# A fused attention and two-layer kernel: the hand-written order of the first half's instructions is replaced

## The chip, the cores and the metric

The kernel runs on one core of one Trainium2 chip. Its time is the device time of one execution in microseconds (us); where several runs were made, their median is compared. A core has five instruction streams that matter here: TensorE (PE; its weight loads are shown as PEld), VectorE (DVE), ScalarE (ACT), GpSimd (POOL) and SyncE (SP), which issues every DMA of this kernel. Each engine takes its own instructions strictly in their order and waits on semaphores for the others.

## What is computed

From the reference, cut to what matters:

```python
# q, k, v: (8, 8, 576, 64); keys and values are averaged over groups of 8 rows
k_p = k.reshape(B, H, 72, 8, D).mean(axis=3)
v_p = v.reshape(B, H, 72, 8, D).mean(axis=3)
attn = softmax(q @ k_p.T / sqrt(D))
x = (attn @ v_p)                 # as 4608 tokens x 512
h = x @ w_in                     # 512 -> 1024
solu = h * softmax(h)
ln = (solu - mean) / sqrt(var + 1e-6) * g_ln
x2 = ln @ w_out                  # 1024 -> 512
h2 = x2 @ w_in2                  # 512 -> 2048
out = (h2 * sigmoid(h2)) @ w_out2    # 2048 -> 512
```

All of it is float32. The kernel splits each float32 operand of a product into a high part, rounded for TensorE's fast format, and a low part (the remainder), and sums three products: high with high, high with low, low with high. The three projections after the hidden layer are done by a seven-product scheme on 2 x 2 blocks, which needs sums and differences of blocks beforehand.

## The kernel before

The 4,608 tokens are 36 tiles of 128. In the **first half** a tile passes through scores, softmax, transposed probabilities, attention, the hidden layer, its normalisation, a transpose and (by groups of four tiles) the first output projection. The weights are unpacked, scaled and split into high and low parts in the same stretch. The **second half**, from the function `window` (L1107) on, is the last two projections; its order comes from loops with slot numbers and is not touched here.

The order of the first half is written out by hand in a text, `SCRIPT` (L62 to L215): 2,881 words, and `run` (L1476) goes through them. A word names a piece of work and its place, such as `S3` (scores of tile 3). Each function behind a word is a generator; each time its word comes up, it emits its next piece, mostly one instruction or a few on one engine, and stops. Since all five engines are under `manual_schedule` (L1439), the instructions of each engine are run in just the order in which the words emitted them. Between engines only the data, the buffers and the semaphores order them. A suffix chooses the engine of that piece where there is a choice: `/1` VectorE, `/2` ScalarE, `/3` GpSimd; without one the piece's default stands (`pick`, L279).

The words (L1468) that the prediction speaks of, with their pieces:

- `W` (warm, L1442): that many pairs of 128x128 filler matmuls on TensorE, whose result nobody reads. `W29` is 58 instructions, `W14` 28, `W6` 12, `W4` 8, `W9` 18.
- `L` (L1347) loads a row of w_in (512 KB), `l` (L1336) unpacks it: ScalarE, then ScalarE or VectorE, VectorE, the high part, the low part. `H` needs it.
- `k` (prep_k, L400): the load of keys (SP; for batch 0 one load of 576 KB serves two head pairs, else 288 KB each), the sum over groups of 8 (VectorE one reduction, or GpSimd three adds, `pool_sum` L386), and scaled copies into `kbd`, two for each of the four head pairs. `v` (L427) and `r` (L455) do the same for the values; loads of batch 0 are 512 and 384 KB, else 256 and 192.
- `q` (L489): the load of one tile's queries (256 KB) into one of three buffers. A buffer is free again when the scores of its tile are done.
- `S` (scores, L496): eight matmuls (sixteen where a tile crosses a batch), then the row maximum on VectorE.
- `X` (softmax, L521): four pieces of two exponentials on ScalarE, a scale, a reciprocal on VectorE, the probabilities `pb` and `lf` (GpSimd by default, or VectorE).
- `T` (L560): transposes on TensorE and the split into high and low. `a` (attend, L606): the attention products, and the split of their result into `xTh` and `xTl`.
- `H` (hidden1, L643): three matmuls of 512 columns. `M` (L665), `E` (L674), `Z` (L689): maximum, exponential, product and mean, variance and scaling; GpSimd has one piece in `E` and two or three in `Z`. `N` (L718): the transpose back.
- `R` (operand1, L746): a difference where the scheme needs one (VectorE or GpSimd), the high part (any of three engines) and the low part `np` (VectorE or GpSimd), for each of two halves. `P` (project1, L790): twice 12 matmuls, then an eviction on VectorE.
- `o` (L1397) and `w` (L331): unpacking of the other weights. `c` (L1448) and `d` (L1456): the first operands of the second half, tokens and weights. `f` (first_pair, L1072): the second half's first seven products and their evictions.

One queue issues all loads and stores in the script's order: a load that waits for its buffer holds back every later one. Keys and values of batches after the first share three raw buffers (`RAWS`, L216).

Of the kernel before, what the change touches and what calls it, by code (L numbers as in the profile page):

```python
# [74 lines left out]
X5 X4 T4 T4 v1,3 T3 r1,1 H1,0,2 X5 T3 k2,2 H1,0,0 T3 q7 T4/1 X5 H1,0,1 T3 k2,0 k2,1/3 X5 o0
S6 v2,0 X5 v2,1 o0 X5 H1,0,3 w0 S6 q8 H1,1,1 X5 T4 T4 X6 T4 E0 H1,1,3 X6 k2,2 H1,1,0 X6 o0
k2,3 H1,1,2 X6 o0/1 a2 a2 M1 o0 o0 a2 o0/3 a2 a2 a2 E1 o0/3 a2/1 a2 a2 S7 o0/3 Z0 E1 a2 q10
o0 S7 a2 o0/3 a2 a2 a2 H2,0,1 a2 H2,1,0 o0 T4/1 H2,1,2 T4 T4 X7 X7 Z0 k2,3 H2,0,2 X6 X7 Z0
a2 v2,2 H2,1,3 r1,1 v2,0 X7 H2,1,1 E1 v2,1 v2,3 Z0/2 H2,0,0 r1,1/1 o0/1 o0/3 o0 r1,1/2
H2,0,3 Z1 Z1 o0/1 T5 o0/3 o0/1 X6 M2 N0 o0/3 N0 N0 X6 o1 E2 T5 T5/1 r2,0 T4 T5 X6 T6 E2 T6  # L80
o0 T6 S8 X7 Z1 o0 T6 H3,0,2 k2,3/2 N0 S8 H3,0,0 E2 Z1 Z2 T6/1 H3,0,1 v2,3 Z2 H3,1,2 v2,2 T5
k3,0 o1 r1,1 r2,0 H3,1,1 k3,1 o0/3 k2,3/2 T6 o1 H3,1,0 k3,2 Z2 q11 X8 H3,0,3 o1 X8 H3,1,3
o1/1 o1 N0 Z2 T5 X8 a3 a3 M3 X8 N1 v2,3 k3,0/3 N1 N1 a3/1 N2 k3,1 E3 S9 k3,2/3 r2,1 r1,1/2
r1,1/1 a3 a3 a3 v3,0 E3 N2 X8 a3 k3,3 X8 a3 a3 a3 a3 E3 X8 Z3 a3 a3 a3 H4,1,2 H4,0,0 a3/1 Z3
a3 N1 H4,1,3 v2,3 S9 v2,3 H4,0,2 o1 Z3 X8/1 o1/1 H4,1,1 X9 X7 r2,1 w2 H4,0,3 X9 X7 k3,3 v3,1
Z3/2 H4,0,1 o1 k4,0 H4,1,0 X9 X7 T7 M4 X9 v2,3 N2 T8 o1/3 T8 k3,3/1 N2/1 o1 o1 E4 v3,0/3 T7
# [1562 lines left out]
```

## Time and profile before

| | |
|---|---|
| median of 3 runs | 1278.84 us (1278.65 to 1280.33) |
| the profiled execution | 1281.28 us |
| its span, first to last instruction | 1279.5 us |
| mean granted TensorE clock | 0.993 |
| PE busy | 1242.0 us (97%), 7,292 matmuls |
| DVE busy | 1016.8 us (79%) |
| ACT busy | 794.1 us (62%) |
| POOL busy | 480.7 us (38%) |

Busy time is the union of the instructions' spans on an engine. In a timeline a row merges equal instructions in a run (x8), and gives in brackets how long the engine was idle before it and what released it. A wait for several semaphores is put down to the one that came last. PEclk is the TensorE clock that was granted, as a share of 2.4 GHz; 0.5 is 1.2 GHz. "m" are products of the second half's first projection, "op" of its second, "hp" hidden, "sp" scores, "av" attention, "xq" the first output projection, "np" its operands.

### The profile page before, as it was taken

Reading aid. Unit: us, or ns where it says so; the run is one execution under the profiler, and the core shown is the slowest. Engines: PE = TensorE matmul, PEld = TensorE weight load, DVE = VectorE, ACT = ScalarE, POOL = GpSimd, SP = SyncE. Lnnn points to the kernel's source line nnn. Section 1 sums busy time; section 2 is a strip of 40 time slices with the busy share of each in tenths; the row PEclk is TensorE's granted clock in tenths of the full one; section 3 lists DMA queues with packets and bytes.
Section 4 is the critical chain, followed back from the end, with each engine's and each line's share of the span. In section 5 each row is a group of like instructions: output and inputs, shape, how many; then the busy total and the mean of one; then the engine's idle time right before and its main releaser. Section 6 shows DMA issues by size and latency. Waiting matters only on the chain.

```text
span 1279.5 us, 21818 instructions
## 1 busy us (share of the span) xinstructions
PE 1242.0 (97%) x7292; PEld 1131.2 (88%) x7292; DVE 1016.8 (79%) x1719; ACT 794.1 (62%) x1949; POOL 480.7 (38%) x655
## 2 busy tenths in 40 slices
...
GB/s 283 215 174 262 215 297 241 247 242 217 195 215 154 99 149 91 201 128 206 281 282 275 231 347 299 239 241 206 367 343 393 329 280 282 254 277 264 197 286 143
DMA packets 139410, 308.69 MB, mean 241 GB/s; under 512 B 12032, under 2 KB 63232, under 8 KB 137760
## 3 DMA queue, kind: packets, MB, share of 16 engines
...
q8 instruction: 58, 0.95, 0.3%
...
## 4 chain that ended last, share of the span: by engine, by line
PE 52%; DVE 2%; DMA 1%; issue 0%; SPq 0%; ACT 0%; DVEq 0%; ACTq 0%
PE m L1057 27%; PE op L1300 24%; DVE gr L851 1%; PE xq L799 1%; DMA gr<-gd 1%; DVE gt L851 1%; SPq L1217 0%; DVE w2s L851 0%; DVE ob L1333 0%; DVE t L851 0%; DVE np L292 0%; ACT gt L1280 0%; ACT np L285 0%; DVE lnr L759 0%; DVE xo L807 0%
## 5 line engine op out<-in xcount | busy, mean ns | idle before, releaser
L1057 PE MATMUL m<-t,w2s 128*128 128x384 f32 x2016 | 351.9, 335 | 2.1 <-DVE gb L1068 2.1
L1057 PEld LDWEIGHTS m<-t,w2s 128*128 128x128 f32 x2016 | 351.0, 189 | 2.8 <-DVE gb L1068 2.4
L1300 PE MATMUL op<-gt,w2o 128*128 128x512 f32 (+1 forms) x1680 | 346.2, 368 | 0.7 <-DVE gt L851 0.5
L1300 PEld LDWEIGHTS op<-gt,w2o 128*128 128x128 f32 x1680 | 292.4, 189 | 54.4 <-DVE gt L851 2.2
L1280 ACT ACTIVATE gt<-gr 128x512 fp32r<-128x512 f32 (+1 forms) x240 | 139.8, 588 | 144.6 <-PE op L1300 55.8
L851 DVE TENSOR_TENSOR gt<-gr,gt 128x512 fp32r<-128x512 f32 (+1 forms) x240 | 155.4, 654 | 61.4 <-ACT gt L1280 57.9
L656 PE MATMUL hp<-w1ih,xTh 128*128 128x512 f32 x288 | 118.7, 412 | 2.7 <-DVE e L681 2.5
L799 PE MATMUL xq<-np,w1p 128*128 128x256 f32 x864 | 113.3, 284 | 4.2 <-DVE np L292 2.8
L656 PE MATMUL hp<-w1ih,xTl 128*128 128x512 f32 x288 | 113.5, 394 | 0.4 <-DVE xTl L292 0.4
L799 PEld LDWEIGHTS xq<-np,w1p 128*128 128x128 f32 x864 | 106.7, 189 | 7.6 <-DVE np L292 4.0
L656 PE MATMUL hp<-w1il,xTh 128*128 128x512 f32 x288 | 112.9, 392 | 0.1
L526 ACT ACTIVATE pr<-sp,st 128x72 f32<-128x72 f32 x288 | 88.6, 329 | 20.7 <-DVE st L517 14.2
L799 PE MATMUL xq<-np,w1o 128*128 128x256 f32 x648 | 84.5, 284 | 2.4 <-DVE np L292 1.1
L799 PEld LDWEIGHTS xq<-np,w1o 128*128 128x128 f32 x648 | 80.1, 189 | 5.4 <-DVE np L292 2.0
L851 POOL TENSOR_TENSOR tt<-x2r 128x768 f32<-128x768 f32 x22 | 44.6, 2028 | 98.0 <-DMA x2r<-x2d 64.9
L851 DVE TENSOR_TENSOR gr<-gr 128x512 f32<-128x512 f32 (+1 forms) x120 | 80.1, 669 | 0.2
L292 POOL TENSOR_TENSOR np<-lnr,np 128x512 fp32r<-128x512 f32 x43 | 60.2, 1401 | 43.1 <-ACT np L285 23.6
L292 DVE TENSOR_TENSOR np<-lnr,np 128x512 fp32r<-128x512 f32 x83 | 65.1, 792 | 10.7 <-ACT np L285 7.2
L656 PEld LDWEIGHTS hp<-w1ih,xTl 128*128 128x128 f32 x288 | 54.2, 188 | 13.1 <-DVE xTl L292 1.1
L1068 DVE TENSOR_TENSOR gb<-m,u 128x384 f32<-128x384 f32 x48 | 26.7, 556 | 49.1 <-ACT u L1124 31.9
L656 PEld LDWEIGHTS hp<-w1ih,xTh 128*128 128x128 f32 x288 | 54.5, 189 | 12.2 <-DVE e L681 4.6
L1068 DVE TENSOR_TENSOR ga<-m,u 128x384 f32<-128x384 f32 x47 | 26.1, 555 | 49.3 <-PE m L1057 49.0
...
## 6 DMA issues: line engine op xcount, KB each, us to landing
...
```

Of the source, the lines that this page charges most:

```text
L292: pick(1).tensor_tensor(lo, src, hi.bitcast(F32), op=ALU.subtract)
L526: nc.scalar.activation(pr[:, g, h], sv[:, g, h], AF.Exp, bias=st[:, 0, g, h : h + 1], accum_out=st[:, 1, g, h : h + 1],)
L656: nc.tensor.matmul(hp[:, f], l, r, start=(n == 1 and m == 0), stop=(n == KC and m == 2))
L799: nc.tensor.matmul(hq[:, b], w[:, k, l], t[:, k % 2, r], start=(b == k == i == 0), stop=(k == 3 and i == 2), skip_group_check=True,)
L851: eng.tensor_tensor(dst, a, b, op=ALU.subtract)
L1057: nc.tensor.matmul(to, wt[:, a, o : o + P], tk[:, b, k], start=(start and k == 0 and m == 0), stop=(k == 1 and m == 2), skip_group_check=n ...
L1068: eng.tensor_tensor(dst, a, b, op=ALU.add)
L1280: nc.scalar.activation(ring[m][:, 0], src, AF.Copy)
L1300: nc.tensor.matmul(acc[c, x][d], w[:, l, P * d : P * d + P], t[:, r], start=(first and f == i == 0), stop=(f == NF - 1 and i == 2), skip_g ...
```

## The change

Only the text of `SCRIPT` is replaced. The new one has 2,881 words too, and each word without its suffix comes up as often as before; the order and the suffixes differ nearly everywhere. The first eight lines and the last two of either text:

```diff
 SCRIPT = """
-L0,0 k0,0 W14 L0,2 k0,2 q0 L0,1 q1 q6 W6 l0,0 L0,3 W29 k0,0 k1,0 l0,0/1 k0,1 l0,2 k0,1/3
-k0,1/1 l0,0 l0,2/1 k0,0/1 k0,0 l0,2 k0,2 l0,2 k0,3 k0,2 k0,2/1 k0,3/1 k0,3/3 S0 l0,1 S0 q2
-k1,1 S1,1 l0,0/1 X0 v0,0 l0,1/1 v0,2 l0,2 X0 W4 r0,0 S1,1 L1,3 X0 X0 l0,0 v1,0 X1 l0,1 X1
-l0,1/1 q3 l0,1 X0 X1 S2 k1,0 X1 X0 v1,1 X1 X0/1 l0,3 L1,2 X0 W9 L1,0 S2 v0,0/3 k1,1 X2 v0,2
-X2 v0,1/3 T0 X2 r0,0 k1,2 T0 T0 r0,1 k1,0/3 X2 X1 L1,1 r0,1/1 v0,3 r0,1 X2 l1,3 w0 X1 T0
-l1,3 S3 r0,1/2 X1 l1,3 l0,3 v0,3/1 r0,1/1 v0,3/1 v0,3 l0,3 l1,2 a0 v0,3 S3 T0 r0,1/2 r0,1/2
-l1,3/3 T0 a0 X3 v1,0 v1,1/3 l0,3 a0/1 k1,3 k1,2 k1,0 o0 a0 a0 a0 q4 k1,2/3 l1,3 q5 l0,3/3
-a0/1 v1,2 a0 a0 a0 a0 X3 v1,3 a0 a0 a0 T1 T1 T1 l1,0 a0/1 H0,0,2 X2 a0 X2 l1,1 l1,1/1 a1 T1
...
-d d d P8,7 R8,4 R8,3 R8,3 R8,3 P8,3 R8,4 R8,4/3 R8,4 P8,5 R8,4 P8,3 d R8,4 P8,4 P8,7 P8,7
-P8,4 P8,3 P8,3 f P8,4 d P8,4 f f d d f f f c f f f f f f f f f f
+L0,0 k0,0 W29 k0,2 q0 q1 L0,1 L0,2 v0,0 l0,0 l0,0/1 v0,2 k0,0 q6 k0,0/1 k0,0 l0,0 k0,3 k0,2/3
+k0,1 k0,1 k0,1/3 k0,2 k0,3/1 k0,3/1 k0,2/1 S0 l0,0/1 l0,0/3 S1,1 l0,1 S0 q2 k1,0 W14 X0 L1,3
+l0,1/1 r0,0 l0,1 X0 k1,1 l0,2 l0,2/1 l0,1/3 X0 v0,0 q3 l0,1/3 X0 v0,1 W6 S1,1 X0 L1,0 X0 l0,2 X1
+X0 v0,2 X1 S2 L1,1 X1 k1,0 k1,2 X0 W4 X1 l0,2/3 S2 k1,0 T0 X1 l1,3 X1 L0,3 T0 v0,3 X1 W9 X2 r0,0
+v1,0 X2 k1,0/3 v0,3/3 r0,1 o0 X2 v0,3 X2 X1 l1,3/1 r0,1 S3 X2 v0,3 T0/1 r0,1 l1,3 a0 r0,1 k1,1
+l1,3 X2 v0,3/1 k1,3 X2 T0 T0 r0,1/2 l1,1 q4 L1,2 r0,1/2 T0 a0 r0,1/2 l1,3/3 S3 l1,1 a0 k1,2 a0
+a0 a0 a0 X3 v1,1 l1,1 a0 a0 a0 a0 l0,3 l1,1/3 l0,2 l0,3 X2 v1,0 l1,1/3 l0,3 v1,2 a0 a0 a0 T1 T1
+H0,0,2 T1 X3 T1 T1 a0 X3 a1 l0,3/3 T1 a1 X3 k1,3 l0,3/3 l1,0 a1/1 v1,3 a0 l1,0 a1 a1 a1 v1,1
...
+P8,2 d d d R8,7 P8,7 D8,2,1 R8,3/3 P8,6 R8,4 P8,7 R8,3 R8,3 R8,3 P8,3 R8,4 R8,4 R8,4/3 R8,4 R8,4
+P8,4 P8,5 d P8,3 d d P8,7 P8,4 P8,7 P8,3 P8,3 P8,4 f c P8,4 f f d c c f f f f f f f f f f f f f
 """
```

At the front, `W14` and `W6` go from ahead of `W29` to behind `S0`, one of batch 0's key sums (`k0,2/3`) goes to GpSimd, and the second key load, the query loads and the value loads `v0,0` and `v0,2` come earlier in SP's order than the third and fourth rows of w_in. Over the whole text the low part of `R` is on GpSimd 53 times of 126 (43 before), the probabilities `pb` 30 times of 36 (26 before), the sums in `k` 8 times of 32 (5 before), those of the main values in `v` 4 times of 32 (11 before); the first copies of `T` and `a` go to ScalarE 71 times of 128 (59 before). At the end, three pieces of `c` instead of one come behind the first `f`.

## Rows read from the trace of the kernel before

**Rows 1.** The chain that ended last, in order of time: start us, us, what.
```profile
562.17 0.60 DVE w2r L851
...
594.78 335.00 PE m L1057 x1920
...
965.45 311.03 PE op L1300 x1529
```

**Rows 2.** Timeline, 574 to 600 us: start us, us, engine line op out<-in.
```profile
575.78 16.89 PE L1057 MATMUL m<-t,w2s 128*128 128x384 f32 x96
575.98 0.69 DVE L807 TENSOR_TENSOR xo<-xq,xo 128x512 f32<-128x512 f32 x1 [0.63 <-PE xq L799]
...
579.17 0.95 DVE L851 TENSOR_TENSOR t<-tt,t 128x768 fp32r<-128x768 f32 x1
```

**Rows 3.** Stretch, us; busy PE, PEld, DVE, ACT, POOL (instructions); PEclk, DMA share, GB/s.
```profile
14.00:50.00 36.00, 26.70 (x156) 23.02 (x155) 28.79 (x59) 26.13 (x116) 21.38 (x33) 0.81 0.79 256
50.00:178.70 128.70, 118.68 (x670) 98.84 (x671) 120.51 (x254) 115.68 (x408) 104.35 (x211) 1.00 0.69 219
178.70:534.30 355.60, 349.13 (x2391) 319.06 (x2390) 311.96 (x544) 207.06 (x579) 211.09 (x302) 1.00 0.60 192
534.30:575.80 41.50, 37.43 (x294) 34.95 (x293) 38.03 (x55) 21.10 (x35) 17.53 (x19) 1.00 0.45 147
```

**Rows 4.** Timeline, 0 to 34 us (PEld is the weight load beside PE).
```profile
1.86 12.92 PE L1445 MATMUL idle<-ident 128*128 128x128 f32 x98 [1.86 <-POOL ident masks.py:199]
...
5.83 0.75 DVE L388 TENSOR_REDUCE kp<-early 128x72 f32<-128x576 f32 x1 [5.83 <-DMA early<-kT]
...
11.68 0.42 DVE L398 TENSOR_SCALAR kbd<-kp 64x72 f32<-64x72 f32 x2
...
14.61 2.13 PE L507 MATMUL sp<-kbd,q 128*128 128x144 f32 x16
15.79 0.33 SPq L491 DMA_DIRECT2D q<-qT  x1
...
29.85 2.26 PE L507 MATMUL sp<-kbd,q 128*128 128x144 f32 x8 [6.54 <-DMA q<-qT]
...
32.34 0.48 PE L618 MATMUL av<-pth,vbh 128*128 128x128 f32 x1 [0.24 <-ACT vbh L285]
```

**Rows 5.** What SP's queue waited for, 0 to 60 us: total us, times, longest.
```profile
SPq L491 <- PE sp L507: 6.9, 2, 6.5
```

**Rows 6.** Busy us in stretches of 4 us at the start, as rows 3.
```profile
0.00:4.00 4.00, 2.14 (x10) 2.15 (x11) 0.00 (x0) 1.28 (x1) 3.43 (x13) 1.00 0.53 160
4.00:8.00 4.00, 4.00 (x31) 4.00 (x31) 2.03 (x5) 1.54 (x3) 0.43 (x2) 1.00 1.02 417
8.00:12.00 4.00, 4.00 (x38) 4.00 (x37) 3.86 (x11) 1.52 (x4) 0.19 (x1) 1.00 1.05 406
12.00:16.00 4.00, 4.00 (x37) 4.00 (x37) 0.31 (x2) 0.00 (x0) 0.05 (x1) 1.00 0.30 111
...
24.00:28.00 4.00, 0.00 (x0) 0.00 (x0) 1.34 (x3) 2.37 (x14) 3.04 (x7) 0.74 1.02 315
```

**Rows 7.** VectorE and GpSimd groups, 0 to 600 us: busy us, mean ns
```profile
L292 DVE TENSOR_TENSOR np<-lnr,np 128x512 fp32r<-128x512 f32 x83 | 65.1, 792 | 10.7 <-ACT np L285 7.2 <-POOL np L289 2.5
...
L292 POOL TENSOR_TENSOR np<-lnr,np 128x512 fp32r<-128x512 f32 x43 | 60.2, 1401 | 43.1 <-ACT np L285 23.6 <-DVE np L287 18.7
...
L538 POOL TENSOR_TENSOR pb<-pr,st 128x512 f32<-128x512 f32 x26 | 28.0, 1075 | 11.1 <-DVE st L534 6.2 <-PE pm L566 2.0 <-PE xq L799 1.5
...
L392 POOL TENSOR_TENSOR raw<-raw 128x288 f32<-128x288 f32 x5 | 4.0, 800 | 0.2
...
L392 POOL TENSOR_TENSOR raw<-raw 128x144 f32<-128x144 f32 x5 | 2.3, 451 | 0.4
...
L392 POOL TENSOR_TENSOR kp<-raw 128x72 f32<-128x72 f32 x5 | 2.0, 393 | 0.4
```

**Rows 8.** Waits, 0 to 580 us: total us, times, longest.
```profile
ACT sqd L693 <- POOL ls L685: 18.0, 15, 2.3
```

More of the change, by code (lines that the diff above doesn't have):

```diff
@@ L75 @@
[L75 to L86, printed above, removed]
@@ new lines @@
+H2,1,1 o0/1 Z1/2 o0/1 o0/3 N0 M2 T4 T5 N0/1 N0 S8 X6 T4 o0 o0/3 o0/3 o0 o0/3 o1 E2 X6 T5 r2,0 N0
+E2 k3,0 X7 T5 X6 T6 w0 T6 k2,3 S8 H3,0,2 T6 o0 X7 v2,3 r1,1/2 H3,1,2 E2 r1,1 T6 T6 X8 k3,1
+H3,0,0 o0/3 w1 T5 T5 Z2 H3,1,1 Z2 T5 k2,3 H3,1,0 o0/3 o1 o1/1 H3,1,3 T6 X8 o1 H3,0,1 X8 k3,0
+H3,0,3 o1 o1 a3 r1,1/1 r1,1 X7 k3,2 a3 Z2 X7/1 q11 M3 N1 a3 N0 X8 r2,0/3 a3 k3,1/3 r2,1 N1 N1 E3
+a3 a3 S9 a3/1 a3 a3 a3 E3 N1 Z2/2 v2,3/3 k3,3 a3/1 N1 v2,3 X8 a3 a3 a3 T7 T7 H4,1,2 o1 q12 X8 E3
+k3,2 a3 H4,0,0 X8 Z3 S9 H4,0,2 v3,0 Z3 a3 H4,1,3 X9 Z3 o1/1 H4,1,1 v2,3 T7 o1 H4,0,3 X9 r2,1
@@ new lines @@
+Z7 k4,3/1 o2 H8,1,0 S14 N6 T12 o2 H8,0,0 o2 o2/3 Z7 T11 o2 w3 H8,0,1 k5,0 X13 X14 H8,1,1 T11
+k5,2 Z7 X14 H8,1,2 N6 r4,1 X13 H8,1,3 o2 o2/1 T11/1 T12 T12 o2 X14 T12 X13 N7 X14 M8 N7 X13 T13
+T12 T13 o2/3 T11 T13 S15 T13 o2/3 k5,2 N7 o2/3 o2 T13 E8 T12 T13 N7 o2/3 a6 E8 a6 w3 o2 o3 X14
+a6 v5,0 o2/1 w4 E8 v5,1 w3 q17 a6 a6 a6 H9,1,3 a6 H9,1,1 Z8 Z8 w3 X14 S15 H9,0,3 q18 X14 N3
+H9,0,0 X15 o2 H9,0,2 X15 Z8 k5,1 X15 H9,1,0 a6 o3 o3/1 H9,0,1 Z8/2 o3 H9,1,2 o3/3 o3 v5,2 w5 a6
+X15 a6 M9 a6 a6 a6 a6 S16 E9 v4,3/1 w4/1 v4,3 N8 w6 v4,3 E9 N8 v4,3 a6 N8 r3,1 w4 H10,0,1 N8 E9
@@ new lines @@
+v5,0 H10,1,2 X14 Z9 S16 Z9 k5,3 H10,0,3 o3 H10,0,2 o3/1 r3,1/1 T13 Z9 v5,1 H10,1,0 X15 X16 a6
+k6,0 H10,0,0 o3 N7 H10,1,3 Z9 q19 v5,2 w7 T13 T13 X16 X16 H10,1,1 w5 k6,1 X15 T13 X15 X16 T14
+M10 N9 T14 T14 X15 T15 T14 E10 S17 T14/1 N9 T15 E10 q20 o3 N9 r3,1/2 X16 S17 H11,0,0 X17 o3/1
+o3/3 k5,3/3 o3/3 E10 k5,3 H11,0,3 o3/1 X17 o3 H11,0,2 o3 o3/3 T15/1 w5 H11,1,0 o3/3 X16 X17 T15
+H11,1,1 o3 N9 T15/1 X16 H11,1,2 T15 w6 v5,3 w8 X17 H11,1,3 w5 w4 H11,0,1 T14 X17 Z10 Z10 r3,1
+X16 a7 a7 M11 o3 Z10 o3/1 o3 a7 E11 a7 a7 a7 S18 o3 q21 X17 a7 E11 X17 o3 o3 o3 E11 o3/3 o3/1
@@ new lines @@
+a8 Z14 N13/1 a8 a8 Z14 X20 R2,4 T18 T18 r5,1 H15,1,1 a8/1 v5,3/3 v6,2 H15,1,2 a8 X20 S22 H15,1,3
+N13 X20 M15 P2,3 v5,3 v5,3 T18 v5,3 T18 T18 w11 N13 X22 R2,7 T19 T18 D3,1,0 w11 P2,3 R2,7 r4,1/1
+r4,1/1 r4,1/1 P2,7 D3,1,1 R3,1/3 w11 w14 T19 T19 X22 E15 T19 X21 X22 X22 P2,7 X21 X22 T19 w13
+w13/1 E15 v6,0 E15 S23 w12 w13 w15 R2,4 k7,0 v6,1 H16,0,0 q25 Z15 Z15 X21 R2,4 H16,1,0 R2,4
+H16,1,1 Z14/2 Z15 w12/1 H16,1,2 v6,2 w16 R2,4 H16,1,3 R3,1 Z15/2 R2,4/3 P2,7 N14 H16,0,1 N14
+P2,7 w14 H16,0,2 X22 S23 N14 R3,1/1 P2,4 w12 R3,1/3 P2,3 w14 w12 w13 X23 P2,4 v6,3 w14 X23 w17
@@ new lines @@
+k6,3/1 P2,3 N15 P2,4 R3,2 H16,0,3 N15 N14/1 P2,4 N15 q26 R3,2 R3,2 P3,1 X23 r6,0 R3,5/3 M16 X23
+a9 P3,1 T19 E16 R3,2 r5,1 a9 N15 P3,2 E16 w15 w15 a9/1 P3,1 P3,2 w18 R3,5/1 w14 R3,5 R3,5/3
+R3,5/3 k6,3 r5,1 r5,1/2 X23 D3,4,0 w15 R3,6/3 D3,4,1 v6,3 a9 a9 a9 S24 a9/1 R3,5/3 H17,0,0 X23
+a9 P3,2 a9 a9 E16 a9/1 k7,0/3 a9 a9 a9 T20 T20 S24 T20 H17,0,1 Z16 a9/1 H17,1,0 X23 T20 T21
+T20/1 R3,6 r5,1 H17,0,2 a9 T20 T21 T21 w18 H17,1,1 X22/1 X22 X23 H17,0,3 r5,1/1 X24 T21 R3,6/3
+T22 T21/1 T22 T21 T22 H17,1,2 X24 T22 R3,6/3 H17,1,3 T22/1 X24 T22 a10 X24 a10 M17 Z16 P3,5 a10
@@ new lines @@
+R3,4/1 Z18 T23 X25 H19,0,1 S26 X25 H19,1,0 T23/1 X26 Z18 H19,1,1 T23 R4,1 X25 H19,0,2 X26 R3,4
+X26 R3,4 H19,1,2 X26 H19,0,3 R3,4/1 u1,0 Z18 r6,1 q29 N17 H19,1,3 v7,0 w20 R3,4 v7,1 P3,4 r6,1
+M19 Z18/2 w20 R4,1 P3,4 E19 T23/1 w22 R4,1/1 w17 w20 N18 P3,3 R4,1/3 E19 S27 N18 P4,1 R4,2/1 E19
+P3,4 Z19 Z19 S27 P3,4 H20,0,0 w20 a10 X27 H20,1,0 R4,2 R4,2/3 Z19 X27 P4,1 T23 w19 Z19/1 w19
+R4,2 N18 X27 w23 H20,1,1 k7,3 v6,3 X27 N19 v6,3 N18/1 v7,2 P4,2 w21 v6,3/3 w19 v6,3 N19/1 w21
+P4,2 P4,1 R4,5 D4,4,0 R4,5 N19 R4,5/3 R4,5 D4,4,1 T24 N19 q30 T24 T24/1 X26 H20,0,1 R4,5/3
@@ new lines @@
+R6,3 R6,3 X35 R6,7 H29,1,2 r7,1/1 P6,6 R6,3/3 X35 H29,1,3 X35 H29,0,0 R6,4/3 r7,1/2 Z28/2 P6,3
+R6,7 T32/1 T33 P6,5 D7,1,0 H29,0,2 R6,7 H29,0,3 R6,7/1 P6,3 M29 R6,7/3 T32 E29 r7,1 N28 D7,1,1
+r7,1 P6,7 X35 N28 E29 P6,7 X34 E29 v7,3 T33 T33/1 X35 T33 H30,0,0 X35 T33/1 N28 T33 r7,1 P6,7
+H30,0,1 N28 X34 Z29 a15 P6,7 a15 P6,3 H30,0,3 Z29 a15 P6,3 a15 a15 a15 H32,0,0,1 R6,4/1 a15
+R6,4/3 R6,4 a15 a15 a15 u0,0 a15/1 a15 a15 a15 T34 Z29 H32,0,1,1 X34/1 T34 T34/1 T35 T34 T34
+Z29/2 H30,1,0 T34 H30,1,1 X35/1 R6,4/1 T35 T35 T35 H30,1,2 R6,4/3 T35/1 H30,1,3 T35 H30,0,2 a16
@@ new lines @@
+a16 M30 H32,1,0,1 N29 a16/1 E30 H32,0,2,1 a16 N29 N29 E30 a16 H32,1,1,1 a16 a16/1 E30 Z30 Z30
+a16 a16 a16 H31,0,0 a16/1 H31,1,0 a16 N29 R7,1/1 a16 a16 Z30 H31,0,1 a16 a16 a15 H31,1,1 a15 c
+H31,1,2 c c Z30/2 H31,1,3 c P6,4 c c c H31,0,2 H32,0,3,1 w30/1 c N30 H31,0,3 R7,1 R7,1/3 P6,4
+R7,1/3 M31 P7,1 E31 R7,2/1 w30 c w30 R7,2/3 R7,2/1 P7,1 E31 N30/1 H32,1,2,1 E31 Z31 Z31 P6,4
+H32,1,3,1 R7,2 P6,4 N30 M32 Z31 P7,2 c E32 H33,0,0 D7,4,0 c H33,1,0 E32 P7,2 Z31/1 H33,1,1 E32
+D7,4,1 Z32 N31 H34,0,0,1 N31/1 H34,0,1,1 P7,1/1 N31 H34,0,2,1 N31 R7,5 H33,0,1 R7,5/1 H33,0,2
@@ new lines @@
+R7,5 R7,5/3 H33,0,3 R7,5/1 P7,2 R7,5/3 H33,1,2 N30/1 H33,1,3 R7,6 H34,1,0,1 R7,6 H34,1,1,1
+R7,6/3 R7,6 M33 R7,6 P7,5 E33 R7,6/3 P7,5 D7,2,0 R7,7 P7,2 Z32 E33 P7,6 R7,3 D7,2,1 Z32 P7,6
+R7,3/3 R7,3/1 R7,3 Z32/2 E33 H34,1,2,1 P7,6 R7,7 H34,1,3,1 Z33 Z33 R7,7/3 R7,7 H34,0,3,1 R7,7
+P7,3 M34 c Z33 R7,7 P7,7 D0,1,0 P7,5 Z33/2 R7,4 P7,7 c c P7,3 R7,4/3 R7,4/3 R7,4 P7,7 R7,4 N32
+P7,3 D0,1,1 H35,0,0 N32 P7,7 R7,4 R0,1 N32 u0,1 P7,4 E34 R0,1 R0,1/1 N32/1 P7,4 E34 R0,1 P0,1
+E34 R0,2/1 Z34 Z34 P7,4 P0,1 R0,2 P7,4 R0,2 R0,2 P0,2 c R0,5 P0,2 D0,4,0 R0,5/1 P0,1 R0,5/3 R0,5
```

211 lines of the change are left out of this document (81 added, 130 removed).

## The prediction

> **What bounds the kernel now.** I read the chain of work that ended last first [rows 1]. Followed back from the last instruction it reaches no further than 562.17 us, and from 594.78 us on it is TensorE almost without a break: 335.00 us of the first projection's products, then 311.03 us of the second's. The script doesn't order that half, so it can only move the moment at which the half begins (the first pair's products, 575.78 us, [rows 2]), and the rest moves with it.
>
> Ahead of that moment the stretches have different limits [rows 3]. From 14 to 50 us no engine is full: VectorE works 28.79 of 36 us, TensorE 26.70. From 50 to 178.7 (attention, hidden layer and weight preparation at once) VectorE is at 120.51 of 128.7 (94%), ScalarE at 115.68, GpSimd at 104.35 (81%). From 178.7 to 534.3 TensorE is at 349.13 of 355.6 (98%), and in the last 41.5 us VectorE (38.03) and TensorE (37.43) share the limit. TensorE's idle time between 50 and 575.8 us is 10.0 + 6.5 + 4.1 = 20.6 us.
>
> The start loses most. TensorE spends 12.92 us from 1.86 on 98 filler matmuls, and the scores of tile 0 start behind them at 14.61 [rows 4]. Their last operand, a scaled key copy on VectorE, was done at 11.68 + 0.42 = 12.10, so the filler outlasted the data by 2.5 us. The next query load on SP's queue needs the buffer that those scores free: it goes out at 15.79, after a wait of 6.5 us [rows 4, 5]. Behind it every other load stands, and the DMA engines run dry: from 12 to 16 us they are busy 0.30, at 111 GB/s against 417 from 4 to 8 [rows 6]. The hole is (1 - 0.30) x 4 = 2.8 us. Later tile 3's scores wait 6.54 us for their queries and start at 29.85; from 24 to 28 us TensorE does nothing, VectorE only 1.34 us, and the granted clock averages 0.74, between its two levels of 2.4 and 1.2 GHz, after TensorE had stood idle. The first attention product starts at 32.34 [rows 4, 6].
>
> **The change part by part.** Both scripts have 2,881 words and the same pieces; only their order and the engine suffixes differ. TensorE's work and SP's transfers keep their sums, so a gain is less waiting and nothing else.
>
> *Filler.* W29 (58 matmuls) now stands alone ahead of S0; W14 and W6 (40) stand between S1 and S2. Ten matmuls run in the first 4 us, 31 in the next 4, then 38 in 4, which is 0.105 us each [rows 6]: 58 end at 8 + 17 x 0.105 = 9.8 us. The data: the second key load is third in SP's queue instead of fourth, with one load of 0.52 MB less ahead, 1.3 us at 417 GB/s. The first key sum began when its load had landed, at 5.83 [rows 4]; 0.59 MB later, at about 7.2, the second lands. One of its two sums goes to GpSimd, three adds of 0.800 + 0.451 + 0.393 = 1.64 us [rows 7], to 8.9; VectorE does three sums of 0.75 from 5.83 on with a weight piece between them, to about 9. With the scaled copies of 0.2 each, S0 starts at about 10.1, 4.5 us sooner. If the data came no sooner than before (12.10) it would be 2.5; if the filler alone held it, 4.8. I take 4.5, since the order of the loads is written out.
>
> *SP's queue.* Ten loads stand ahead of q2 in either order, 4.36 MB before and 4.59 MB now (from the shapes). With 0.64 MB moved in the first 4 us (160 GB/s) and 410 GB/s after, 4.59 MB last until about 13.6 us; q2 goes out at about 11.3, so the hole of 2.8 us closes. The first values (v0) now stand ahead of q2, and q3 is the 16th load with 6.62 MB up to it, not the 18th with 7.40: another 1.9 us. Of tile 3's wait of 6.54 us most should go. Late next is VectorE, busy 28.79 of the 36 us: the stretch can shrink beyond the shift by nothing, or by all its idle time, 7.2 us. I take 2.0, three quarters of its one clear gap (4 - 1.34 = 2.66 us at 24 to 28), since the other gaps are waits on one another. With the shift: **-6.5 us**, ends -2.5 and -12.0.
>
> *Engines changed.* Ten low parts of projection operands go from VectorE to GpSimd (53 there, not 43): -10 x 0.792 = -7.9 us on VectorE, +14.0 on GpSimd [rows 7]. Four scalings of probabilities go the same way: +4.3 on GpSimd (1.075 each), some -3 on VectorE. Seven value sums come back and three key sums go, net four off GpSimd at about 1.64: -6.6, and +3.0 on VectorE. Sums: VectorE about -8, GpSimd +11.7; the other moves nearly cancel. The relief is worth at most VectorE's share in the stretch where it is fullest, 8 x 128.7 / 525 = 2.0 us. GpSimd covers its load even if all of it fell there: 104.35 + 11.7 = 116 of 128.7. If that cover is gone and every moved low part stands on the path, the cost is 10 x (1.401 - 0.792) = 6.1 us. I take 0, ends -2.0 and +6.1.
>
> The row has a low part on GpSimd at 1.77 times VectorE's time, and the rule speaks against the move: the Trainium skill, GPSIMD Engine Reference, section 4.1, keeps elementwise work on VectorE and calls GpSimd about twice as slow with two inputs. By its factor the ten would cost 7.9 us on the path, and the sum would be +1.4 instead of -6.5.
>
> *The order from 50 to 575.8 us.* Here an order can win at most TensorE's 20.6 idle us. Counted in the two scripts, TensorE pieces with a direct producer at most two words ahead fall from 42 to 27, at most four from 62 to 56. That lengthens leads a little; what it is worth no row tells, and the words' spacing is a plan. I take 0, ends -5 and +5, a quarter of the idle time.
>
> *The end.* The low part of T3 now stands behind the first pair's first product. The fourth product needs it, 18 matmuls in, at 575.78 + 18 x 16.89 / 96 = 578.9; VectorE has it after its last eviction (576.7) and 0.95 us [rows 2], at 577.6. It is covered by 1.3 us: 0, or 0.95 if the cover is gone.
>
> **Sum:** -6.5 us. The profiled execution took 1281.28 us (span 1279.5, 1.8 around it), 2.4 above the median of the runs, 1278.84 (1278.65 to 1280.33). Taken off the median it gives **1272.3 us**; a profile as far above the median would show about 1274.8. A measurement of this kernel tells about 0.2%, 2.6 us, from no change.
>
> **Rivals.**
> *The whole start is won* (1266.8): the stretch up to 50 us also loses all of VectorE's idle time, -12.0. For it: tile 3's queries were 6.54 us late and attention begins only at 32.34. Against: VectorE is in demand from 28 us on.
> *Better on average, not on this chip* (1278.8): the order was made for scattered durations, and this kernel has one set of them. The dense stretch takes the 6.5 us back. It spends 128.7 us where its fullest engine works 120.51, so 6.5 more of waiting is possible. Against: its leads are as long as before, and DMA, which keeps its own time, is busy only 0.69 of that stretch [rows 3].
> *GpSimd late for every tile, slower* (1284.9): each of the 36 tiles passes GpSimd three times, for the mean, the variance and the scaling, and ScalarE already waits there 18.0 us in 15 waits for the mean [rows 8]. In GpSimd's queue these short pieces now stand behind more long ones (1.401, 1.075, 1.64). At 0.35 us a tile that is 36 x 0.35 = 12.6, less 6.5: +6.1. It decides from (6.5 + 2.6) / 36 = 0.25 us a tile. Against: GpSimd has 24 idle us in the dense stretch. The Trainium skill, GPSIMD Engine Reference, section 8, adds that GpSimd shares its SBUF interfaces with VectorE, which would slow VectorE's two-input work beside it; no row here separates that.
> *It doesn't do what it says*: the scores of tile 0 start at 12.1 because some load is late; -2.5, and the time is at the edge of no change (1276.3). I count it with the second rival.
>
> **How the numbers follow.** Forecast (1270 to 1276.2) 0.52; whole start won 0.16; taken back or start not won 0.19; GpSimd late 0.13. Faster by over 0.2%: 0.52 + 0.16 = 0.68; within 0.2%: 0.19; slower: 0.13. The range runs from a little below the whole start (1265.5) past no change (1278.8 + 2.6) to 1281.5: it leaves out most of the slower case and a larger win with a better order, together under 0.2.
>
> **What would show it.** Right: scores of tile 0 at about 10 us; DMA busy over 0.8 from 12 to 16; tile 3's scores before 25 and attention before 27; the first pair near 569.3; TensorE's idle time from 50 us to the first pair still near 20 us. Wrong: scores of tile 0 after 12, or the first pair at 575 with the start won (then the dense stretch took it back), or ScalarE's waits for GpSimd well over 18 us.

## The result and the profile after

The changed kernel took **1266.28 us** (median of 4 runs, 1264.8 to 1268.13), the kernel before 1279.59 in the same comparison (1278.65 to 1280.62): a ratio of 0.9897, 95% interval [0.9879, 0.9914], or 13 us. The profiled execution took 1268.13 us with a span of 1266.3, against 1281.28 and 1279.5. So the sign was as forecast and the time lies in the range given, near its lower end; the gain is twice the forecast of 6.5 us.

Lines in the changed kernel are 7 lower, since its text is shorter by seven lines: L1057 is now L1050, L799 is L792, L292 is L285.

The timeline at the end of the first half, of the kernel after, answers to [rows 2]:

```profile
561.68 14.06 PE L1050 MATMUL m<-t,w2s 128*128 128x384 f32 x80
561.88 0.69 DVE L800 TENSOR_TENSOR xo<-xq,xo 128x512 f32<-128x512 f32 x1 [0.54 <-PE xq L792]
562.49 0.95 DVE L844 TENSOR_TENSOR t<-tt,t 128x768 fp32r<-128x768 f32 x1
```

The first pair's products begin at 561.68 us, not at 575.78: 14.1 us sooner. From there to the end it is 704.6 us, 703.7 before. Over all the kernels below this second half, which none of them edits, takes 701.6 to 704.9 us in the profiles, so 0.9 is within the scatter. All of the gain arises ahead of 561.68.

Next the stretches, as [rows 3]. The bounds are the same pieces of work as there: the maximum of tile 0's hidden layer (VectorE's first `ls<-hp`, at 43.54 us), that of tile 12 (172.97), that of tile 35 (522.91), and the first pair. Such a maximum is itself a piece that the two scripts place differently, so the inner bounds are rough by an instruction or two; the first pair is firm.

```profile
10.00:43.54 33.54, 28.83 (x194) 26.40 (x193) 28.40 (x57) 27.28 (x121) 23.86 (x31) 0.90 0.79 271
43.50:173.00 129.50, 118.33 (x673) 99.62 (x672) 119.72 (x247) 116.67 (x417) 110.15 (x212) 1.00 0.76 245
173.00:522.90 349.90, 348.52 (x2396) 319.48 (x2396) 305.79 (x545) 204.66 (x568) 216.97 (x304) 1.00 0.58 189
522.90:561.70 38.80, 35.20 (x286) 33.86 (x285) 36.85 (x52) 21.06 (x36) 17.15 (x17) 1.00 0.47 158
```

Tile 0's maximum comes 6.5 us sooner (43.54 for 50.00). Behind it 7.6 more are won up to the first pair. TensorE's idle time there falls from 20.6 us to 11.2 + 1.4 + 3.6 = 16.2, so 4.4 is waiting that the profile shows. The other 3.2 are busy time: TensorE is busy 502.05 us behind that maximum, 505.24 before, with the same number of matmuls (3,355 in the rows of either kernel); why these take less is not shown. The stretch that changed most is the third: 1.4 us idle of 349.9, where it was 6.5 of 355.6. The dense second one is no better: 11.2 idle for 10.0.

The start, of the kernel after, as [rows 4]:

```profile
1.85 8.54 PE L1438 MATMUL idle<-ident 128*128 128x128 f32 x58 [1.85 <-POOL ident masks.py:199]
5.93 0.75 DVE L381 TENSOR_REDUCE kp<-early 128x72 f32<-128x576 f32 x1 [1.01 <-DMA early<-kT]
7.44 1.32 POOL L385 TENSOR_TENSOR early<-early 128x288 f32<-128x288 f32 x2 [3.26 <-DMA early<-kT]
9.41 0.51 DVE L391 TENSOR_SCALAR kbd<-kp 64x72 f32<-64x72 f32 x3
10.23 2.13 PE L500 MATMUL sp<-kbd,q 128*128 128x144 f32 x16
11.41 0.33 SPq L484 DMA_DIRECT2D q<-qT  x1
12.19 4.63 PE L1438 MATMUL idle<-ident 128*128 128x128 f32 x40
16.92 1.22 PE L500 MATMUL sp<-kbd,q 128*128 128x144 f32 x8
23.13 1.25 PE L500 MATMUL sp<-kbd,q 128*128 128x144 f32 x8 [1.43 <-ACT pr L519]
24.12 0.32 PE L611 MATMUL av<-pth,vbh 128*128 128x128 f32 x1
26.56 0.47 PE L611 MATMUL av<-ptl,vbh 128*128 128x128 f32 x1 [2.12 <-DVE ptl L285]
```

The last scaled key copy is done at 9.92, and the scores follow the 58 matmuls without a pause, at 10.23, so the filler ends last, by some 0.3 us. The query load goes out at 11.41 instead of 15.79. Tile 3's scores start at 23.13 and wait for exponentials on ScalarE (`pr`, 1.43 us), no longer for their queries. In SP's order the value loads `v0,0` and `v0,2` and the load `q6` stand ahead of the fourth row of w_in, but behind the third (`L0,2`), not ahead of both. SP's queue and the stretch of the hole, as [rows 5, 6]:

```profile
SPq L484 <- PE sp L500: 3.3, 1, 3.3
```

```profile
12.00:16.00 4.00, 4.00 (x38) 4.00 (x38) 3.86 (x9) 3.66 (x21) 2.26 (x3) 1.00 1.01 387
```

The DMA share from 12 to 16 us is 1.01, at 387 GB/s: the hole of 0.30 and 111 GB/s is closed. Last the groups, as [rows 7], and ScalarE's wait, as [rows 8]:

```profile
L285 POOL TENSOR_TENSOR np<-lnr,np 128x512 fp32r<-128x512 f32 x53 | 72.7, 1373 | 61.4 <-DVE np L280 41.5 <-ACT np L278 11.4 <-PE hp L649 2.7
L285 DVE TENSOR_TENSOR np<-lnr,np 128x512 fp32r<-128x512 f32 x73 | 56.7, 789 | 1.9 <-ACT np L278 1.3
```

```profile
ACT sqd L686 <- POOL ls L678: 12.7, 9, 2.4
```

GpSimd has ten low parts more and yet holds ScalarE up less at this wait, 12.7 us for 18.0.

### The profile page after: what moved, and what is told of

It is laid out like the page before. It is cut to its first block, busy times and chain, and to the rows that moved or that the text cites. A ratio compares the mean times of both kernels' runs of the same rounds, so it can differ in the third digit from the quotient of the medians.

```text
span 1266.3 us, 21791 instructions
## 1 busy us (share of the span) xinstructions
PE 1237.3 (98%) x7292; PEld 1130.6 (89%) x7292; DVE 1005.5 (79%) x1705; ACT 792.0 (63%) x1954; POOL 497.8 (39%) x656
## 4 chain that ended last, share of the span: by engine, by line
PE 59%; DVE 4%; DMA 4%; ACT 1%; issue 1%; POOL 0%; SPq 0%; DVEq 0%; ACTq 0%; POOLq 0%
PE m L1050 26%; PE op L1293 25%; PE xq L792 3%; PE hp L649 3%; DMA w2o<-wod 1%; DMA gr<-gd 1%; DVE np L285 1%; DMA gd<-gb 1%; DMA lnr<-lnd 1%; PE av L611 1%; DVE xo L800 0%; PE tp L718 0%; DVE t L844 0%; DVE ls L662 0%; PE pm L559 0%
## 5 line engine op out<-in xcount | busy, mean ns | idle before, releaser
L1050 PE MATMUL m<-t,w2s 128*128 128x384 f32 x2016 | 352.2, 335 | 2.8 <-DVE gb L1061 2.2
L1050 PEld LDWEIGHTS m<-t,w2s 128*128 128x128 f32 x2016 | 350.8, 188 | 3.9 <-DVE gb L1061 2.5
L792 PE MATMUL xq<-np,w1p 128*128 128x256 f32 x864 | 112.1, 284 | 2.4 <-DVE np L285 1.7
L792 PEld LDWEIGHTS xq<-np,w1p 128*128 128x128 f32 x864 | 106.1, 189 | 5.2 <-DVE np L285 2.5
L285 POOL TENSOR_TENSOR np<-lnr,np 128x512 fp32r<-128x512 f32 x53 | 72.7, 1373 | 61.4 <-DVE np L280 41.5
L792 PE MATMUL xq<-np,w1o 128*128 128x256 f32 x648 | 84.7, 283 | 1.7 <-issue 1.1
L792 PEld LDWEIGHTS xq<-np,w1o 128*128 128x128 f32 x648 | 80.7, 189 | 3.6 <-issue 1.3
L1061 DVE TENSOR_TENSOR ga<-m,u 128x384 f32<-128x384 f32 x47 | 26.1, 555 | 50.8 <-PE m L1050 50.6
L672 ACT ACTIVATE e<-hp,ls 128x1024 f32<-128x1024 f32 x36 | 40.2, 1116 | 38.4 <-DVE ls L662 37.7
```

The lines of the kernel that those rows point to most:

```text
L285: pick(1).tensor_tensor(lo, src, hi.bitcast(F32), op=ALU.subtract)
L672: nc.scalar.activation(e, hp, AF.Exp, bias=nm, accum_out=sm)
L792: nc.tensor.matmul(hq[:, b], w[:, k, l], t[:, k % 2, r], start=(b == k == i == 0), stop=(k == 3 and i == 2), skip_group_check=True,)
L1050: nc.tensor.matmul(to, wt[:, a, o : o + P], tk[:, b, k], start=(start and k == 0 and m == 0), stop=(k == 1 and m == 2), skip_group_check=n ...
L1061: eng.tensor_tensor(dst, a, b, op=ALU.add)
```

## The experiments

Two things were open: how much comes from the start and how much from the order behind it, and whether the engines of the pieces or their places do it. Each kernel is a script put together from the old one and the new one. The table gives for each the median and the ratio to the kernel before on the same chip (whose median there was 1280.4 to 1282.1 for e1 to e12), and from its profile the start of tile 0's and tile 12's maximum and of the first pair (us).

```
kernel                    median   ratio [95%]              tile 0  tile 12  first pair
before                   1279.59                              50.0    178.7    575.8
after                    1266.28   0.9897 [0.9879, 0.9914]    43.5    173.0    561.7
e1  new to tile 0        1277.63   0.9979 [0.9967, 0.9991]    45.0    173.4    569.0
e2  new from tile 0      1275.52   0.9961 [0.9948, 0.9973]    51.5    183.6    570.9
e3  filler only          1277.53   0.9976 [0.9966, 0.9985]    47.3    176.5    573.3
e4  filler back          1270.58   0.9919 [0.9906, 0.9933]    48.8    178.0    565.4
e5  new to tile 12       1274.60   0.9952 [0.9938, 0.9966]    45.9    175.3    570.5
e6  new from tile 12     1274.59   0.9953 [0.9940, 0.9966]    48.5    181.7    567.9
e7  new order, old eng.  1326.78   1.0359 [1.0344, 1.0374]    47.8    196.7    618.3
e8  old order, new eng.  1330.41   1.0385 [1.0371, 1.0400]    54.1    197.9    625.1
e9  ten low parts back   1267.60   0.9896 [0.9881, 0.9911]    45.3    174.6    561.4
e10 ten low parts forth  1287.61   1.0052 [1.0039, 1.0064]    50.6    179.1    582.1
e11 operands' eng. back  1293.57   1.0097 [1.0083, 1.0111]    44.8    174.9    588.0
e12 filler in the gaps   1266.26   0.9877 [0.9860, 0.9893]    43.6    173.4    561.6
```

All words ahead of tile 0's maximum are the same in before, e6 and e10, and there it starts at 50.0, 48.5 and 50.6. They are the same in after, e5, e9 and e11: 43.5, 45.9, 45.3 and 44.8. One profile's start is thus good to some 1.2 us either way, and the difference of the means is 49.7 - 44.9 = 4.8 us.

From tile 0's maximum to the first pair the table has 516.1 to 519.4 us in the six kernels whose words and engines from tile 12 on are the new ones (after, e2, e4, e6, e12, and e9 with its ten engines put back), and 524.0 to 526.0 in the four that have the old ones there (before, e1, e3, e5). The means differ by some 7 us. TensorE's idle time between tile 12's and tile 35's maximum goes with it: 1.0 to 1.6 us in the six, 4.2 to 6.5 in the four, whatever the start.

The expectations below take tile 0's maximum of the kernel after at 41.5 us and so the start as worth 8.5; the trace has 43.54, so 6.5.

**e1 and e2: cut at tile 0's maximum.** e1 has the new words and engines up to there and then the old ones in their old order, those already used left out; e2 the reverse.

```diff
 H0,1,3 X4 T3 a1
-M0 r1,0/3 S5 k2,1 k2,2 X4
+w0 w1 r1,1 o0 r1,0 a1 M0 o0/3 o0 k2,1 S5
...
```

```diff
 H0,1,3 T2 X4 X3
-M0 T2 o0/3 o0 k2,0 k2,1 q9 S5
+k2,0 q9 T2 T2 k2,0 X4 T3 M0 S5 k2,1
...
```

> New order and engines up to the first tile's maximum, the old order and engines for all pieces that are left. Theory A (two separate sources: the start gives about 8.5 us, fewer waits of TensorE from 171 to 520 us give about 6): scores of tile 0 at 10.2 us, first maximum near 41.5, first pair near 567, time 8.5 us under before, about 1271. Rival B (the later waits are fewer only because everything runs ahead of the loads, so the start alone brings it all): first pair near 562, about 1266.

> Old order up to the first tile's maximum, new order and engines behind it. Theory A: first maximum at 50 us as before, TensorE's waits between tile 12's maximum and tile 35's near 1 us instead of 6.5, first pair near 570, time about 1274. Rival B: waits as before, about 1279.

e1 won 2.7 us (0.0021 of 1280.69), e2 5.0. Both parts count, so the start is not the whole, and neither is what stands behind it: rival B fell. Theory A missed the time of e1 by 6 us and came near that of e2, whose idle time in the third stretch is 1.0 us. The two sum to 7.7 of 13.2. The rest may be the price of a seam, since the words around it were placed for other neighbours; that is not shown. e1's profiled run was the fastest of its twelve (1273.64), so its markers are kinder than its median.

**e5 and e6: cut at tile 12's maximum,** which puts the seam behind the dense stretch.

```diff
 w6 X18 R2,1/3 N10
-M12 S19 N10 Z11 Z11 N10 S19
+N10 N10 Z11 Z11 Z11 M12 P2,1 r4,1/1 w9
...
```

```diff
 X18 N5 X17/1 w6
-M12 X18 P2,1 w6 r4,1/1 a7
+N7 q20 q21 w6 R2,2 X17 k6,1 T16
...
```

> New order up to the maximum of tile 12 (171 us), old order behind it. Theory A: start won, stretch from the first maximum to tile 12 as with the change (about 130 us), the later waits of TensorE as before (6.5 us): first pair near 568.5, time about 1272. Rival C (the late waits depend on the state in which the dense stretch leaves the buffers and queues): waits near 1 us, about 1266.

> Old order up to the maximum of tile 12, new order behind it. Theory A: nothing moves up to 178.7 us; behind it the stretch to tile 35 is 6 to 7 us shorter, time about 1273. Rival C: waits as before, about 1279.

e5 won 6.1 us and e6 6.0, and 12.1 is nearly the whole. So about half comes from the words and engines ahead of tile 12 and half from those behind it, where the prediction had put nothing. Both times are within 3 us of theory A, and rival C fell: TensorE's idle time between the maxima of tiles 12 and 35 is 4.2 us in e5 and 1.6 in e6.

**e3 and e4: the filler alone.** e3 is the old script with `W14` behind the scores of tile 1 and `W6` ahead of those of tile 2; e4 the new one with both ahead of `W29` again.

```diff
-L0,0 k0,0 W14 L0,2 k0,2 q0 L0,1 q1 q6 W6 l0,0 L0,3 W29
+L0,0 k0,0 L0,2 k0,2 q0 L0,1 q1 q6 l0,0 L0,3 W29
...
-q2 k1,1 S1,1 l0,0/1
+q2 k1,1 S1,1 W14 l0,0/1
...
-X0 X1 S2
+X0 X1 W6 S2
```

```diff
-L0,0 k0,0 W29 k0,2
+L0,0 k0,0 W14 W6 W29 k0,2
...
-q2 k1,0 W14 X0 L1,3
+q2 k1,0 X0 L1,3
...
-v0,1 W6 S1,1
+v0,1 S1,1
```

> The old order with one thing moved: W14 and W6 (40 filler matmuls) stand behind the second scores instead of ahead of W29. Theory A1 (filler and load order each do a part): scores of tile 0 wait for the key sums and start near 12.2 us, 2.4 sooner; tile 3's queries still land late; time 2 to 4 us under before, 1275 to 1277. Rival A2 (the filler alone opened the queue, the order of the loads does nothing): first maximum near 42, about 1271.

> The new order with W14 and W6 put back ahead of W29, so that 98 filler matmuls stand ahead of the scores. Theory A1: scores of tile 0 at 14.6 us again; the loads ordered ahead of the third query load are in by then, so attention starts some 2 to 4.4 us later than with the change, time about 1268 to 1271. Rival A2: the whole 8.5 us of the start is lost, about 1275.

Alone it won 3.1 us; put back, it cost 2.8 (0.9919 less 0.9897), though the intervals of e4 and the kernel after just overlap. Tile 0's scores start at 11.1 in e3 and at 15.9 in e4 (12.2 and 14.6 were expected), so 3.5 to 5.7 us at the scores are worth about 3 at the end. Rival A2 fell in both. The filler alone (e3, 3.1 us) wins as much as all words of the new start ahead of the old order (e1, 2.7), so what the order of the loads adds at the end is not shown.

**e7 and e8: order and engines apart.** 459 of the words have another engine in the new script. e7 is the new order with each piece on its old engine, e8 the old order with each on its new one.

```diff
-l0,0 k0,3 k0,2/3 k0,1 k0,1 k0,1/3 k0,2 k0,3/1 k0,3/1
+l0,0 k0,3 k0,2 k0,1 k0,1/3 k0,1/1 k0,2 k0,3/1 k0,3/3
...
```

```diff
-k0,0 l0,2 k0,2 l0,2 k0,3
+k0,0 l0,2 k0,2/3 l0,2/3 k0,3
...
```

> The new order of all pieces with the old choice of engine for each. Theory D (order alone, engines don't matter, as the prediction's sum had them at nothing): about 1266 to 1268. Rival E (the 8 us less on VectorE are what shortens the waits): the waits of TensorE for VectorE come back, about 1271 to 1273. If GpSimd's extra load had a price that the order hides: below 1265.

> The old order with the new choice of engine for each piece. Theory D: near before, 1278 to 1281, since a low part on GpSimd (1.40 us) in a place planned for VectorE (0.79) makes a few projections wait. Rival E: 1273 to 1276, since VectorE has 8 us less to do.

Both theories fell: e7 is 46 us slower than before and e8 49. The loss is spread; e7's stretches from tile 0's maximum to the first pair, with the columns of [rows 3]:

```profile
47.80:196.70 148.90, 124.53 (x677) 104.76 (x676) 124.04 (x257) 117.41 (x409) 105.29 (x210) 0.95 0.66 213
196.70:574.80 378.10, 354.80 (x2377) 319.37 (x2375) 316.38 (x541) 203.47 (x573) 209.73 (x305) 1.00 0.53 173
574.80:618.30 43.50, 39.54 (x299) 37.29 (x298) 35.52 (x56) 21.45 (x36) 13.20 (x15) 0.96 0.45 151
```

TensorE is idle 24.4, 23.3 and 4.0 us in them, against 11.2, 1.4 and 3.6 in the kernel after: 35.5 us of the 52.3 by which these stretches are longer; the rest is busy time. Everything comes a little late: from 60 to 560 us the largest rows of TensorE's waits are spread over five kinds of products and the results of three engines:

```profile
PE hp L644 <- DVE e L669: 5.5, 8, 1.3
PE xq L787 <- POOL np L280: 4.2, 3, 3.0
PE pm L554 <- POOL pb L526: 3.9, 1, 3.9
PE tp L713 <- ACT e L693: 3.1, 3, 1.7
PE av L606 <- DVE ptx L587: 2.9, 3, 1.6
```

**e9, e10 and e11: the price of a piece's engine.** Of the low parts that went from VectorE to GpSimd ten were picked, spread from tile 12 to tile 35. e9 puts them back in the new script; e10 moves the same ten in the old script; e11 gives all pieces of the projection operands their old engines in the new order.

```diff
-H12,1,0 w6 X18 R2,1/3 N10 M12 S19
+H12,1,0 w6 X18 R2,1 N10 M12 S19
...
```

```diff
-N9 X18 X18 R2,1 w5 X18
+N9 X18 X18 R2,1/3 w5 X18
...
```

```diff
-w10 w8 S21 R2,5/3 v5,3
+w10 w8 S21 R2,5 v5,3
...
-a8 Z14 X20 R2,4 T18
+a8 Z14 X20 R2,4/3 T18
...
```

> The new order and engines, but ten low parts of projection operands, spread from group to group, are back on VectorE (GpSimd has 43 of 126, as before; VectorE 7.9 us more, GpSimd 13.7 us less). Theory F, what the prediction assumed: each piece has a price by its engine, and GpSimd's low part is 0.6 us longer; the ten are worth nothing to 6 us on the path, so the time is 1260 to 1266 beside a kernel after of about 1266. Theory H: VectorE's relief is what the change won in the middle stretch; then without the ten 2 to 7 us are lost, 1268 to 1273. Theory G: engine and place are one plan, and each piece that is changed alone costs about 46 us / 459 = 0.1 us, so ten cost 1 us, 1266 to 1268.

> The old order and engines, but the same ten low parts go from VectorE to GpSimd. Theory F: the operands come 0.6 us later each, 0 to 6 us slower than before, 1281 to 1287. Theory H: VectorE's relief is won here too, 2 to 7 us faster, 1274 to 1279. Theory G: about 1 us slower, 1280 to 1283.

> The new order, with the old engine for every piece of the projection operands (156 pieces of 459 that differ) and the new engine for all others. Theory G: 156/459 of the 60 us between the kernel after and the new order with all old engines, that is 20 us, so about 1286. Theory F: GpSimd has ten low parts fewer, nothing else of size, 1260 to 1268. A third, G2: the operands are what TensorE waits for most, and nearly all of the 60 us comes from them, 1310 to 1326.

e9: 0.9896 for 0.9897, no difference, with intervals of some 2 us either way. e10: 6.7 us slower (0.0052 of 1280.41), just past theory F's end, where theory H wanted a gain. So the relief of VectorE by these ten pieces (theory H) is not what won. The same ten moves cost nothing that shows in the one order and 0.67 us each in the other. e11 costs 26 us against the kernel after (0.0200), 43% of what all 459 engines cost there, with 34% of the words; theory G is nearest, some way off.

The view of the operands' tile `np` says who waited for it (us, times), from 178 to 575 us. In the kernel before:

```profile
  PEld xq L799: 8.0, 14
  PE xq L799: 5.1, 11
```

In the kernel after:

```profile
  PEld xq L792: 3.8, 7
  PE xq L792: 2.9, 6
```

With the ten back on VectorE (e9):

```profile
  PEld xq L786: 2.9, 6
  PE xq L786: 2.1, 4
```

With the ten on GpSimd in the old order (e10):

```profile
  PEld xq L787: 11.1, 18
  PE xq L787: 7.3, 14
```

PEld is the weight load beside the products, so its waits mostly are theirs a second time. The products wait 2.9 us for operands in the new order although more of these come from the slower engine, 5.1 in the old, and 7.3 once ten of the old order's low parts are made slower. These 2.2 us are part of e10's loss: from tile 12's maximum to the first pair its profile is 5.9 us longer, 3.8 of them idle time of TensorE.

In the new order those ten words stand where their result is not yet wanted. Since every engine runs its pieces in the script's order, each of the ten can be found in the traces. In the kernel after nine of them end 0.9 to 8.3 us before the first matmul that reads them, and one 0.1 before; in e10 five of the ten end 0.05 us before it. One of them is the second low part of `R1,4`, which the eighth matmul of its product reads. In the kernel after it ends at 357.25, and that matmul starts at 359.91 (the second row is another low part, on VectorE):

```profile
355.97 1.28 POOL L285 TENSOR_TENSOR np<-lnr,np 128x512 fp32r<-128x512 f32 x1 [0.75 <-ACT np L278]
356.14 1.65 DVE L285 TENSOR_TENSOR np<-lnr,np 128x512 fp32r<-128x512 f32 x1
359.07 1.59 PE L792 MATMUL xq<-np,w1p 128*128 128x256 f32 x12
```

In e10 it is the later of two on GpSimd, and the product stops for it after seven matmuls:

```profile
373.55 3.04 POOL L280 TENSOR_TENSOR np<-lnr,np 128x512 fp32r<-128x512 f32 x2 [1.69 <-DVE np L275]
376.65 2.03 PE L787 MATMUL xq<-np,w1p 128*128 128x256 f32 x15 [0.43 <-POOL np L280]
```

**e12: does the clock hold up the start?** In the kernel before the granted clock is 0.50, the lower of its two levels, from 26 to 38 us, after TensorE did nothing from 24 to 28. The kernel after, in stretches of 2 us:

```profile
24.00:26.00 2.00, 0.43 (x5) 0.28 (x3) 1.94 (x5) 1.41 (x4) 1.32 (x2) 1.00 1.03 396
26.00:28.00 2.00, 1.44 (x7) 1.43 (x7) 1.91 (x4) 1.77 (x5) 1.91 (x2) 0.53 1.01 389
30.00:32.00 2.00, 2.00 (x9) 1.74 (x9) 1.90 (x5) 1.71 (x6) 2.00 (x4) 0.50 0.41 144
```

There it is low from 26 to 33 us. e12 is the kernel after with 32 filler matmuls more, in its two gaps:

```diff
-X1 W9 X2 r0,0
+X1 W15 X2 r0,0
...
-r0,1 S3 X2 v0,3
+r0,1 S3 W10 X2 v0,3
```

> The kernel after with 32 filler matmuls more, in the two gaps of the start: the nine pairs ahead of tile 3's scores become fifteen, and ten new pairs follow those scores. In the kernel after TensorE idles at 21.7 to 23.1 and at 24.4 to 26.6 us, and the granted clock is 0.50 from about 26.2 to 33.0 us. Theory C (TensorE's clock limits that stretch): no gap, no fall, and of the 6.4 us of products between 26.6 and 33.0 half is won: marker of tile 0's hidden layer near 28 instead of 31.1, maximum of tile 0 near 38.5 to 39.5 instead of 41.5, time 1263 to 1264 beside about 1266.3 of the kernel after. Theory V (VectorE, busy 3.84 and 3.90 of 4 us from 24 to 32 us, limits it): the clock stays up, the time does not move, 1265.5 to 1267.5. Theory X: the filler itself stands ahead of products that were ready, 1267.5 to 1270.

```profile
24.00:26.00 2.00, 2.00 (x20) 2.00 (x19) 1.94 (x5) 1.69 (x5) 1.77 (x3) 1.00 1.04 399
26.00:28.00 2.00, 2.00 (x20) 1.98 (x18) 1.91 (x4) 1.83 (x8) 1.65 (x2) 1.00 0.98 367
30.00:32.00 2.00, 0.96 (x3) 0.38 (x3) 1.98 (x4) 2.00 (x12) 2.00 (x4) 1.00 0.50 169
```

The clock stays at its upper level through 32 us, and TensorE then stands idle half of 30 to 32, as its timeline in e12 shows:

```profile
29.90 0.50 PE L649 MATMUL hp<-w1il,xTh 128*128 128x512 f32 x1
31.44 0.49 PE L649 MATMUL hp<-w1ih,xTl 128*128 128x512 f32 x1 [1.04 <-DVE xTl L285]
```

The low part `xTl` that it waits for is made by VectorE, busy 1.98 of those 2 us (ScalarE and GpSimd are full there too). Tile 0's maximum starts at 43.61 for 43.54 and the median is 1266.26 for 1266.28: theory V. Against its own runs of the kernel before the ratio is 0.9877 [0.9860, 0.9893], and the two intervals overlap, so this isn't shown to be a faster kernel than the kernel after.

## Why the prediction was right, and where it was off

*Filler.* Scores of tile 0 were put at 10.1 and came at 10.23, in part by luck. GpSimd's sum from 7.44, VectorE's and the scaled copies went as written, to 9.92 for about 10.1; but the filler, put at 9.8, ran until the scores began and held them. The term was mis-sized: 4.5 us at the scores are about 3 at the end (e3, e4). The forty matmuls only moved: they now stand ahead of tile 2's scores, which gain 19.2 - 16.9 = 2.3 us.

*SP's queue.* The hole closed as written, attention began at 24.12, its second product at 26.56 (before 27 was asked), and tile 3's scores at 23.13 (before 25). For the whole start -6.5 was forecast; the two profiles show -6.5 at tile 0's maximum, and the four against three profiles with equal words -4.8. What it is worth at the end is between e1's 2.7 and e5's 6.1, which has the dense stretch too. VectorE was late next, as written: e12 shows the wait on it. Its idle time was not used up, though: 33.54 - 28.40 = 5.1 us of it remain from 10 to 43.54, where 7.2 stood from 14 to 50: 2.1 went, as the 2.0 that was taken.

*The order from 50 to 575.8 us* was taken as 0, with ends of 5 either way, and **this is the step that failed**. New words and new engines together were worth 7.6 us there in the profile, and 6.0 from tile 12 on by e6. A sign stood in the prediction: by its count the 42 pieces of TensorE with a producer at most two words ahead had become 27. I set it aside because no row priced a word of lead. But TensorE was full to 98% in the middle stretch, and its 6.5 us of waits there were all short, 1.4 us at most, so small shifts of the producers could remove nearly all of them. That the longer leads did it is not shown: e7 has the same words in the same order and so the same leads, and TensorE idles 23.3 us in that stretch. The view that shows the short waits is that of TensorE's waits between tile 12's and tile 35's maximum. The kernel before, with the four largest of its nine rows:

```profile
PE xq L799 <- DVE np L292: 1.7, 4, 0.6
PE pl L572 <- DVE ptx L599: 1.4, 1, 1.4
PE hp L656 <- DVE e L681: 0.6, 1, 0.6
PE xq L799 <- DVE ptx L599: 0.5, 1, 0.5
...
```

The kernel after, all of its rows:

```profile
PE tp L718 <- DVE e L700: 0.4, 1, 0.4
PE xq L792 <- DVE np L285: 0.4, 1, 0.4
PE av L611 <- DVE xo L800: 0.3, 1, 0.3
```

Nor was the gain "less waiting and nothing else", as the prediction has it: up to the first pair TensorE's idle time falls by 9.0 us (31.7 to 22.7), and its busy time by 5.1.

*Engines changed* was taken as 0 and is 0 within the noise for the ten low parts (e9), in the order that they were placed for. The upper end, 6.1 if every one stands on the path, is what the old order makes of them (6.7, e10). But the step treated engines and order as two terms to be added, and e7 and e8 show that they aren't: each alone costs 46 to 49 us, together they win 13. The Trainium skill, GPSIMD Engine Reference, section 4.1, calls two-input work on GpSimd about twice as slow and keeps it on VectorE. The rows have 1373 ns to 789, 1.74 times. In the old order the rule gives the right answer; in the new one the slower piece has room, 0.9 us or more for nine of the ten, and the rule's cost doesn't appear.

*The end.* Nothing waits for the late low part: the first pair's products run on through it in the timeline above. A wait that was not foreseen comes behind them, 0.51 us at 576.26 for a weight operand (`w2s`) on VectorE.

*The rivals.* "The whole start is won" named nearly the measured time (1266.8), but by a mechanism that did not happen: more than half of the gain is elsewhere (some 7 us of 13) and most of VectorE's idle time is still there. That the time lies in the range is to that extent luck, since its lower end was put there for that rival. "Better on average, not on this chip" fell; the dense stretch gave back 0.7 us (129.43 for 128.69 between the two maxima), not 6.5. "GpSimd late for every tile" fell too: ScalarE's wait is 12.7 us, below 18.0. Of the signs named, TensorE's idle time from tile 0's maximum on was to stay near 20 us and fell to 16.2, and the first pair was to come near 569.3 and came at 561.68; both signs speak for a gain behind the start.

Open is why a cut at tile 0 loses 5 us of the sum where one at tile 12 loses 1, and which property of the new plan makes TensorE's waits in the middle stretch so few.
